# A hashed-attention and maxout feed-forward kernel: bits issued from GpSimd's queue, new due units for the reciprocal chain, feed-forward from unit 11, weight parts from unit 2

## The chip, the cores and the metric

The kernel runs on one core of one Trainium2 chip. The metric is the device time of one execution in microseconds (us). A core has TensorE (PE: matmuls, and PEld: loading their weights), VectorE (DVE), ScalarE (ACT), GpSimd (POOL) and SyncE (SP, which here only issues DMAs). Each engine works its instructions off in the order in which the program gives them. A DMA issued by SP or by POOL waits in that engine's queue until what it waits for is there, and everything behind it in the same queue waits too.

## The reference

Attention with a hash mask over 4 batches of 8 heads, sequence 768, head size 64; then a feed-forward layer with the maximum of three products.

```python
q_bits = (np.einsum('bhsd,dk->bhsk', q, proj) > 0)        # 6 bits, k_bits likewise
mask = q_bucket[:, :, :, None] == k_bucket[:, :, None, :]  # equal bits
scores = np.where(mask, scale * np.matmul(q, k.transpose(0, 1, 3, 2)), -1e9)
attn = softmax(scores)
x = np.matmul(attn, v)            # then to (B * S, H * D) = (3072, 512)
h = np.maximum(np.maximum(x @ w1, x @ w2), x @ w3)         # 512 -> 768
out = h @ w_out                                            # 768 -> 512
```

## The kernel before, in words

**Pairs and units.** Heads are worked in 16 pairs (`pi`), four to a batch; `jj` is the pair's place in its batch. A pair has 12 units, so a batch has 48 and the kernel 192. A unit (`scores`, L271) is two matmuls (L276) over 128 keys each and one exponential on ACT (L279). The mask is part of the matmul: below the 64 rows of the head lie 6 rows of bits as +0.5 or -0.5 in `S`, so that pairs with unequal bits get a large negative term.

**Preparing a pair** (`prep_groups`, L132). Four `tgroup`s transpose k and q on TensorE (L149) and copy them to `T2` (L157, L159). The first of a pair also issues the k and q loads of the next pair on POOL (`begin`, L114). `hashes` multiplies by `proj` (L193), makes `bits` on DVE (L196) and issues four DMAs that put the bits into `S` (L202). POOL then casts the even half of `S` (L205, `even`), DVE the odd half (L208). Pair 0 has its own way: `hash_first` (L178) and `bits_first` (L181), where DVE writes the bits into `S` without a DMA. Preparation goes on some units ahead: the hashes of pairs 2 to 6 fall on units 15, 26, 35, 45 and 56, and are used from units 23, 35, 47, 59 and 71.

**The values and the reciprocal chain.** After a pair's half (6 units) or whole (12 units), `values` (L302) multiplies by v (L298), sums the exponentials (L312), and DVE writes `avs` and `ys` (L321, L323). The sums must be inverted and spread over partitions, by `normalize` (L329), in four steps: `gather` (SP, L344, `dd<-ys`) at once, then `invert` (DVE L347 and L348, then SP L349, `rd<-rr`), `spread` (SP L353, `rb<-rd`, two DMAs) and `scale` (POOL L357, `xT<-avs,rb`). The last three come due so many units later, as a list of (units, step) says. A step is put into the program at the end of its due unit. What is left after unit 191 is sorted by its due number and placed among the last feed-forward groups, by a running count `at` of their costs.

**Feed-forward** (`ffn_groups`, L216). A batch gives 36 groups of four matmuls (L226, cost 0.66; DVE takes the maximum, L231 and L233) and 6 groups of six matmuls (L239, cost 1.32; ACT copies, L249, SP stores, L250). The first half of the groups reads the first query half of `xT`, all four pairs of it. The groups of batch b start `FFN_AT` units into batch b + 1, at 0.66 a unit; the last batch's come behind the loop.

**Other orders of the loop.** v is loaded on POOL (L121) and cast there (L124). The 15 weight parts are issued on POOL one at a time (L391) at units 8, 12, ..., 64.

Of the kernel before, what the change touches and what calls it, by code (L numbers as in the profile page):

```python
# [12 lines left out]
AluOp = mybir.AluOpType  # L13
# [4 lines left out]
def kernel(  # L18
# [12 lines left out]
    nc = tc.nc  # L31
    B, H, S, D = q.shape
    NBITS = proj.shape[1]
    P = 128
    NCH = S // P

    HALF = S // 2
# [4 lines left out]
    NPAIR = B * HPAIR  # L42
    KR = D + NBITS
# [64 lines left out]
    def load(pi, eng):  # L108
        b, jj = divmod(pi, HPAIR)
        nats = [nat.tile([P, 2, NCH * D], FP32, tag=nm, name=nm) for nm in ("qnat", "knat")]  # L110
        for h0, nh in ((0, 1), (1, 1)) if pi == 0 else ((0, 2),):
            for side in (1, 0):
                h = 2 * jj + h0
                eng.dma_start(nats[side][:, h0 : h0 + nh, :],  # L114
                                  (q, k)[side][b, h : h + nh].rearrange("h (p c) d -> p h (c d)", p=P))
        natural[pi] = nats
# [9 lines left out]
    weight_parts = []  # L126
# [5 lines left out]
    def prep_groups(pi):  # L132
        st = {}

        def begin():
            st["T2"] = t2pool.tile([P, 2, 2, HALF], FP32, tag="T2", name="T2")
            st["S"] = spool.tile([KR, 2, 2, 2, HALF], BF16, tag="S", name="S")
            trans[pi] = st["S"]
            if 1 < pi + 1 < NPAIR:
                load(pi + 1, nc.gpsimd if pi > 1 else nc.sync)  # L140

        def tgroup(side, hd):
            def go():
                if not st:
                    begin()
                mp = ms_ps.tile([P, 512], FP32, tag="ms", name="mp")
                n = natural[pi][side]
                for i in range(CH2):
                    nc.tensor.transpose(mp[:, i * P : (i + 1) * P], n[:, hd, 2 * i * D : (2 * i + 2) * D], iden[:])  # L149
                o = st["T2"][:, side, hd, :]  # L150
                if pi == 0 and (hd, side) != (0, 1):
                    if side == 0:
                        nc.scalar.mul(o, mp[:, 0:HALF], QS)
                    else:
                        nc.scalar.copy(o, mp[:, 0:HALF])
                elif side == 0:
                    nc.vector.tensor_scalar(out=o, in0=mp[:, 0:HALF], scalar1=QS, scalar2=None, op0=AluOp.mult)  # L157
                else:
                    nc.vector.tensor_copy(o, mp[:, 0:HALF])  # L159
                if pi == 0:  # L160
                    nc.gpsimd.tensor_copy(st["S"][0:D, side, hd, 0, :], o[0:D])
            return go

        def odd_first(hd):
            for side in (1, 0):
                o, i_ = st["S"][0:D, side, hd, 1, :], st["T2"][D : 2 * D, side, hd, :]
                if hd == 0:
                    nc.scalar.copy(o, i_)
                else:
                    nc.vector.tensor_copy(o, i_)  # L170

        first_bp = {}

        def hash_first(hd):
            for side in (1, 0):
                bp = first_bp[side] = ms_ps.tile([P, 512], FP32, tag="ms", name="bp")
                for par in range(2):
                    nc.tensor.matmul(bp[32 * par : 32 * par + 32, 0:HALF], pj[:, 1 + par, :], st["T2"][:, side, hd, :],  # L178
                                     start=True, stop=True)

        def bits_first(hd):  # L181
            for side in (1, 0):
                for par in range(2):
                    nc.vector.tensor_scalar(out=st["S"][D:KR, side, hd, par, :],
                                            in0=first_bp[side][32 * par : 32 * par + NBITS, 0:HALF],
                                            scalar1=0.0, scalar2=0.5, op0=AluOp.is_gt, op1=AluOp.subtract)

        def hashes():
            bp = ms_ps.tile([P, 512], FP32, tag="ms", name="bp")
            for side in range(2):  # L190
                for hd in range(2):
                    g = 2 * side + hd
                    nc.tensor.matmul(bp[32 * g : 32 * g + 32, 0:HALF], pj[:, 0, :], st["T2"][:, side, hd, :],  # L193
                                     start=True, stop=True)
            bits = bpool.tile([P, HALF], BF16, tag="bits", name="bits")
            nc.vector.tensor_scalar(out=bits[:], in0=bp[:, 0:HALF], scalar1=0.0, scalar2=0.5,  # L196
                                    op0=AluOp.is_gt, op1=AluOp.subtract)
            for hd in range(2):
                for side in (1, 0):
                    p0 = 32 * (2 * side + hd)  # L200
                    eng = nc.gpsimd if pi == 1 and hd == 1 else nc.sync
                    eng.dma_start(st["S"][D:KR, side, hd, :, :], bits[p0 : p0 + 2 * NBITS, :])  # L202

        def even():
            nc.gpsimd.tensor_copy(st["S"][0:D, :, :, 0, :], st["T2"][0:D])  # L205

        def odd(side):
            return lambda: nc.vector.tensor_copy(st["S"][0:D, side, :, 1, :], st["T2"][D : 2 * D, side])  # L208

        if pi == 0:  # L210
            return [tgroup(1, 0), tgroup(0, 0), lambda: odd_first(0), lambda: hash_first(0), lambda: bits_first(0),
                    tgroup(1, 1), tgroup(0, 1), lambda: odd_first(1), lambda: scores(0), lambda: scores(1),
                    lambda: hash_first(1), lambda: bits_first(1)]
        return [tgroup(s, h) for h in (0, 1) for s in (1, 0)], hashes, [even, odd(1), odd(0)]

    def ffn_groups(b):  # L216
# [45 lines left out]
    UPB = NU // B  # L262
    UPG = NCH
    UPP = 2 * UPG
    WEIGHTS_AT = 8
    FFN_AT = 13
    EARLY_CH = 4
    PAIRS_AT = UPB + UPP
    xts, avs_of, ys_of = {}, {}, {}
# [59 lines left out]
    def normalize(pi, q0, nq):  # L329

        b, jj = divmod(pi, HPAIR)
        if jj == 0:
            xts[b] = xpool.tile([P, NJC, S], FP16, tag="xT", name="xT")
        xt, avs, ys = xts[b], avs_of[pi], ys_of[pi]
        G = 16
        W = nq * HALF // G
        dd = small.tile([2 * G, 2, 2 * HALF // G], FP32, tag="dd", name="dd")
        rr = small.tile([2 * G, 2 * HALF // G], FP32, tag="rr", name="rr")
        rd = drp.tile([2 * G, W], FP32, tag=f"rd{nq}", name="rd")
        rb = rbpool.tile([P, 2, HALF], FP32, tag="rb", name="rb")  # L340

        def gather():
            for half in range(2):
                nc.sync.dma_start(dd[:, half, 0:W], ys[32 * half : P : D, q0 : q0 + nq, :])  # L344

        def invert():
            nc.vector.tensor_add(rr[:, 0:W], dd[:, 0, 0:W], dd[:, 1, 0:W])  # L347
            nc.vector.reciprocal(rr[:, 0:W], rr[:, 0:W])  # L348
            nc.sync.dma_start(rd[:, :], rr[:, 0:W])  # L349

        def spread():
            for hd in range(2):
                nc.sync.dma_start(rb[hd * D : (hd + 1) * D, 0:nq, :],  # L353
                                    rd[hd * G : (hd + 1) * G, :].rearrange("(o p) i -> o (p i)", o=1).to_broadcast((D, nq * HALF)))

        def scale(i):
            return lambda: nc.gpsimd.tensor_mul(xt[:, jj, (q0 + i) * HALF : (q0 + i + 1) * HALF],  # L357
                                                avs[:, q0 + i, :], rb[:, i, :])

        gather()  # L360
        if nq == 1:
            return [(7, invert), (10, spread), (15, scale(0))] if pi < NPAIR - 1 else [(4, invert), (4, spread), (4, scale(0))]
        return [(8, invert), (11, spread)] + [(18, scale(i)) for i in range(nq)]

    with tc.manual_schedule():
        wm = ms_ps.tile([P, 512], FP32, tag="ms", name="wm")
# [16 lines left out]
        for u in range(NU):  # L383
            pi = units[u][0]
# [2 lines left out]
                cast_v[pi + 1] = load_v(pi + 1, nc.gpsimd)  # L387
            if u % UPP == 10 and pi + 1 < NPAIR:
                cast_v[pi + 1]()
            if u >= WEIGHTS_AT and u % 4 == WEIGHTS_AT % 4 and weight_parts:  # L390
                nc.gpsimd.dma_start(*weight_parts.pop(0))  # L391
            if ub == FFN_AT and b > 0:
                ffn += ffn_groups(b - 1)
# [7 lines left out]
            else:  # L401
                fill = slot in (2, 3, 5) if u < UPB + FFN_AT else slot in (1, 4)
            if fill:
                if hash_ready and u < PAIRS_AT:
                    do_hash()
                elif prep and prep[0][0] < pi + AHEAD:
                    _, i, g, hs = prep.pop(0)
# [25 lines left out]
        at = 0  # L433
# [35 lines left out]
```

## Time and profile before

| What | Value |
|---|---|
| Median of 3 runs | 315.08 us (312.65 to 316.27) |
| The profiled execution's own time | 314.91 us |
| Its span, first to last instruction | 313.1 us |
| PE, ACT, DVE, POOL busy | 291.7, 182.4, 195.6, 109.9 us |
| Mean granted TensorE clock | 0.978 |
| DMA | 35.88 MB, mean 115 GB/s |

The span is the time on which the rows of the profile lie; the profiled execution took 1.8 us more than it. A row of a timeline has the start in us, the length in us, the engine, the line, the operation, what it writes and reads, how many instructions were merged, and in brackets how long the engine stood idle before it and for whom. The granted clock is the share of full speed at which TensorE was allowed to run. A row "SPq" or "POOL ... DMA_DIRECT2D" is the issue of a DMA, not its transfer.

### The profile page before, as it was taken

The numbers are of one execution on the slowest core, as the hardware profiler recorded it, in microseconds if no ns is written. First come the engines' busy times: TensorE is split into PE (matmuls) and PEld (weight loads), VectorE is DVE, ScalarE is ACT, GpSimd is POOL, SyncE is SP. The second block draws the span as 40 slices with busy tenths as digits, with TensorE's granted clock in tenths as the row PEclk, the third lists the DMA queues.
The fourth block names the chain that finished last, engine by engine and source line by source line (L and its number), as shares of the span: only waits on it lengthen the run. The fifth ranks groups of instructions, "written<-read, shape, count | busy, mean of one in ns | idle before, by whom it ended". The sixth has DMA issues, their size and how long they took to land.

```text
span 313.1 us, 6752 instructions
## 1 busy us (share of the span) xinstructions
PE 291.7 (93%) x2593; PEld 161.8 (52%) x2593; DVE 195.6 (62%) x419; ACT 182.4 (58%) x222; POOL 109.9 (35%) x131
## 2 busy tenths in 40 slices
PE   8999989895999999999999999999999999469994
PEld 3454445442565566555656566555655555236562
DVE  2867557765478387746876497836763558038481
ACT  3787888882565946584757756683849572200201
POOL 2387545686707061215617070235130200130000
PEclk9999999997799999999999999999999999969999
DMA  7548779397924432245415440233111300410202
GB/s 206 197 89 230 155 160 224 81 250 196 244 85 137 146 122 67 56 144 166 158 51 159 153 129 33 55 98 115 53 54 56 104 2 17 129 61 0 103 0 100
DMA packets 19491, 35.88 MB, mean 115 GB/s; under 512 B 4960, under 2 KB 11700, under 8 KB 19460
## 3 DMA queue, kind: packets, MB, share of 16 engines
q0 software_dynamic: 7200, 19.29, 22.7%
q1 hardware_dynamic: 11956, 16.04, 16.5%
q8 instruction: 20, 0.33, 0.4%
q10 hardware_dynamic: 304, 0.13, 0.2%
q14 instruction: 11, 0.09, 0.1%
HBM read 31.46 MB, written 6.39 MB: 121 GB/s over the span
## 4 chain that ended last, share of the span: by engine, by line
PE 76%; DMA 9%; ACT 5%; DVE 3%; issue 2%; SPq 2%; POOL 1%; POOLq 0%; ACTq 0%; DVEq 0%
PE l L226 28%; PE sc L276 17%; PE av L298 9%; PE l L239 7%; PE mp L149 5%; ACT AT L279 4%; PE sm L312 4%; DMA S<-bits 3%; PE bp L193 3%; DMA rd<-rr 3%; DMA rb<-rd 2%; PE wm L368 1%; SPq L353 1%; PE bp L178 1%; SPq L202 1%
## 5 line engine op out<-in xcount | busy, mean ns | idle before, releaser
L279 ACT ACTIVATE AT<-sc,bias_t 128x768 f16<-128x768 f32 x192 | 167.3, 905 | 75.0 <-PE sc L276 70.8
L226 PE MATMUL l<-xT,w_sb 128*128 128x384 f16 x576 | 113.7, 333 | 10.4 <-POOL xT L357 9.7
L276 PE MATMUL sc<-S 70*128 70x384 bf16 x384 | 91.6, 328 | 5.4 <-ACT AT L279 4.3
L226 PEld LDWEIGHTS <-w_sb 128*128 128x128 f16 x576 | 57.0, 99 | 48.7 <-issue 15.1
L357 POOL TENSOR_TENSOR xT<-avs,rb 128x384 f16<-128x384 f32 x32 | 31.7, 1005 | 142.9 <-DMA rb<-rd 120.6
L233 DVE TENSOR_TENSOR ht<-ht,l 128x384 f16<-128x384 f16 x96 | 52.7, 549 | 17.8 <-PE l L226 13.2
L276 PEld LDWEIGHTS <-S 70*128 70x128 bf16 x384 | 34.5, 98 | 44.1 <-issue 24.6
L231 DVE CAST ht<-l 128x384 f16<-128x384 f32 x48 | 26.6, 553 | 30.1 <-PE l L226 29.1
L249 ACT COPY osb<-l 128x512 f32<-128x512 f32 x23 | 13.6, 589 | 45.6 <-PE l L239 45.2
L298 PE MATMUL av<-AT,vo 128*32 128x385 f16 x768 | 38.9, 329 | 0.0
L239 PE MATMUL l<-wout_sb,ht 128*128 128x512 f16 x144 | 34.0, 379 | 0.0
L298 PEld LDWEIGHTS <-vo 128*32 128x32 f16 x768 | 17.5, 96 | 17.5 <-issue 9.8
L205 POOL CAST S<-T 64x1536 bf16<-64x1536 f32 x15 | 22.0, 1466 | 12.6 <-DVE T L157 12.6
L157 DVE TENSOR_SCALAR T<-mp 128x384 f32<-128x384 f32 x30 | 16.5, 549 | 14.2 <-PE mp L149 13.7
L159 DVE COPY T<-mp 128x384 f32<-128x384 f32 x31 | 17.2, 554 | 12.7 <-PE mp L149 11.5
L208 DVE CAST S<-T 64x768 bf16<-64x768 f32 x30 | 21.7, 731 | 0.5
L239 PEld LDWEIGHTS <-ht 128*128 128x128 f16 x144 | 14.0, 97 | 15.0 <-DVE ht L233 0.4
L312 PE MATMUL sm<-AT,ones 128*32 128x384 f16 x384 | 21.1, 325 | 0.0
L321 DVE TENSOR_SCALAR avs<-av,sv 128x384 f32<-128x384 f32 x32 | 19.8, 618 | 1.6
L323 DVE TENSOR_SCALAR ys<-sm 128x384 f32<-128x384 f32 x32 | 17.5, 548 | 0.0
L149 PE MATMUL mp<-iden,knat 128*128 128x128 f32 x96 | 16.3, 279 | 0.3 <-DMA knat<-in_k_dram 0.2
L149 PE MATMUL mp<-iden,qnat 128*128 128x128 f32 x96 | 16.1, 277 | 0.1
(42 smaller groups left out, 157.0 us busy)
## 6 DMA issues: line engine op xcount, KB each, us to landing
out_dram<-osb SPq DMA_DIRECT2D x23, 256.0 KB
vnat<-in_v_dram POOLq DMA_DIRECT2D x15, 384.0 KB, 4.4
knat<-in_k_dram POOLq DMA_DIRECT2D x13, 384.0 KB, 4.3
qnat<-in_q_dram POOLq DMA_DIRECT2D x13, 384.0 KB, 4.7
rb<-rd SPq DMA_DIRECT2D x24, 192.0 KB
w_sb<-in_moe_w_dram POOLq DMA_DIRECT2D x12, 192.0 KB, 5.8
rb<-rd SPq DMA_DIRECT2D x16, 96.0 KB
S<-bits SPq DMA_DIRECT2D x58, 9.0 KB
```

The lines of the kernel that those rows point to most:

```text
L149: nc.tensor.transpose(mp[:, i * P : (i + 1) * P], n[:, hd, 2 * i * D : (2 * i + 2) * D], iden[:])
L205: nc.gpsimd.tensor_copy(st["S"][0:D, :, :, 0, :], st["T2"][0:D])
L208: return lambda: nc.vector.tensor_copy(st["S"][0:D, side, :, 1, :], st["T2"][D : 2 * D, side])
L226: nc.tensor.matmul(ps[:, 0:HALF], w_sb[wi][:, jc, fb * P : (fb + 1) * P], xb[:, jc, hf * HALF : (hf + 1) * HALF], start=(jc == 0), stop=(j ...
L231: nc.vector.tensor_copy(hts[fb][:], ps[:, 0:HALF])
L233: nc.vector.tensor_tensor(out=hts[fb][:], in0=hts[fb][:], in1=ps[:, 0:HALF], op=AluOp.max)
L239: nc.tensor.matmul(ps[:, 0:DM], hts[fb][:, tb * P : (tb + 1) * P], wout_sb[:, fb, :], start=(fb == 0), stop=(fb == NFB - 1))
L276: nc.tensor.matmul(sc[:, j, 0:HALF], th[0:KR, 1, hd, j, kp * P : (kp + 1) * P], th[0:KR, 0, hd, qh, :], start=True, stop=True)
L279: nc.scalar.activation(at[:, :, 0:HALF], sc[:, :, 0:HALF], ActFn.Exp, bias=bias_t[:], scale=SCALE)
L298: nc.tensor.matmul(av[p0 : p0 + 32, 0 : HALF + 1], vones[pi][:, hd, d0 : d0 + 32], at[:, c % 2, 0 : HALF + 1], start=(c == 0), stop=(c == ...
L312: nc.tensor.matmul(sm[32 * t : 32 * t + 32, 0:HALF], ones[:, :], at_of(qh, hd, c)[:, c % 2, 0:HALF], start=(s == 0), stop=(s == CH2 - 1))
L357: return lambda: nc.gpsimd.tensor_mul(xt[:, jj, (q0 + i) * HALF : (q0 + i + 1) * HALF], avs[:, q0 + i, :], rb[:, i, :])
```

## The change

The bits of a pair go out on POOL's queue instead of SP's, except those of pair 1's first head. In `bits_first` the four operations become six, the k side cut at column 128, in another order. The due units of the chain depend on the pair's place: 4, 7, 11 for the last pair of a batch (was 7, 10, 15), 4, 6, 8 for the last pair of all (was 4, 4, 4), 8, 13, 18 for the first two of a batch and 6, 9, 14 for the third (both were 8, 11, 18). Feed-forward starts at unit 11 of the next batch instead of 13; the same constant moves the unit from which preparation takes fewer slots, from 61 to 59. The weight parts go at units 2, 4, 6, 8, then 12 to 52 by 4.

```diff
         def bits_first(hd):
-            for side in (1, 0):
-                for par in range(2):
-                    nc.vector.tensor_scalar(out=st["S"][D:KR, side, hd, par, :],
-                                            in0=first_bp[side][32 * par : 32 * par + NBITS, 0:HALF],
-                                            scalar1=0.0, scalar2=0.5, op0=AluOp.is_gt, op1=AluOp.subtract)
+            for side, par, lo, hi in ((1, 0, 0, P), (1, 1, 0, P), (0, 0, 0, HALF), (1, 0, P, HALF), (1, 1, P, HALF),
+                                      (0, 1, 0, HALF)):
+                nc.vector.tensor_scalar(out=st["S"][D:KR, side, hd, par, lo:hi],
+                                        in0=first_bp[side][32 * par : 32 * par + NBITS, lo:hi],
+                                        scalar1=0.0, scalar2=0.5, op0=AluOp.is_gt, op1=AluOp.subtract)
...
-                    eng = nc.gpsimd if pi == 1 and hd == 1 else nc.sync
+                    eng = nc.sync if pi == 1 and hd == 0 else nc.gpsimd
                     eng.dma_start(st["S"][D:KR, side, hd, :, :], bits[p0 : p0 + 2 * NBITS, :])
...
-    WEIGHTS_AT = 8
-    FFN_AT = 13
+    WEIGHTS_AT = (2, 4, 6, 8) + tuple(range(12, 56, 4))
+    FFN_AT = 11
...
         if nq == 1:
-            return [(7, invert), (10, spread), (15, scale(0))] if pi < NPAIR - 1 else [(4, invert), (4, spread), (4, scale(0))]
-        return [(8, invert), (11, spread)] + [(18, scale(i)) for i in range(nq)]
+            return [(4, invert), (6, spread), (8, scale(0))] if pi == NPAIR - 1 else [(4, invert), (7, spread), (11, scale(0))]
+        at = (8, 13, 18) if jj < 2 else (6, 9, 14)
+        return [(at[0], invert), (at[1], spread)] + [(at[2], scale(i)) for i in range(nq)]
...
-            if u >= WEIGHTS_AT and u % 4 == WEIGHTS_AT % 4 and weight_parts:
+            if u in WEIGHTS_AT:
                 nc.gpsimd.dma_start(*weight_parts.pop(0))
```

## The prediction

> **What bounds the kernel now.** I read the page first, then the busy time by stage, then the chain that ended last, and the timelines of POOL and of the DMA queues around the two places where the chain leaves TensorE.
>
> ```profile
> span 313.1 us, 6752 instructions
> PE 291.7 (93%) x2593; PEld 161.8 (52%) x2593; DVE 195.6 (62%) x419; ACT 182.4 (58%) x222; POOL 109.9 (35%) x131
> PEclk9999999997799999999999999999999999969999
> ```
>
> TensorE is the engine to beat, and its clock falls twice, near 72 to 86 us and near 274 to 281 us. By stage (PE, PEld, DVE, ACT, POOL busy, granted clock, DMA share, GB/s):
>
> ```profile
> 9.20:72.00 62.80, 58.49 (x623) 29.01 (x624) 43.30 (x88) 52.56 (x64) 41.01 (x51) 1.00 0.69 170
> 76.00:262.00 186.00, 184.32 (x1716) 107.28 (x1719) 122.03 (x255) 120.73 (x144) 61.77 (x67) 0.98 0.33 102
> 73.00:76.00 3.00, 0.20 (x3) 0.01 (x1) 1.12 (x3) 0.00 (x0) 1.05 (x2) 0.80 0.84 287
> 76.00:81.50 5.50, 5.50 (x18) 2.63 (x18) 2.18 (x4) 0.90 (x1) 4.12 (x6) 0.50 0.66 152
> 269.50:276.90 7.40, 0.53 (x4) 0.23 (x3) 0.41 (x2) 0.58 (x1) 2.03 (x3) 0.72 0.28 99
> ```
>
> There are four stages. In 9 to 72 us (units 0 to 60, no feed-forward) ScalarE paces at about 1.02 us a unit, and DMA and POOL are well filled. In 76 to 262 us TensorE is full at 1.43 us a unit. Between them lies a hole of 3 us, and a second of 7 us stands before the last feed-forward. Who ends the holes:
>
> ```profile
> 74.95 0.98 POOL L357 TENSOR_TENSOR xT<-avs,rb 128x384 f16<-128x384 f32 x1 [2.59 <-DMA rb<-rd]
> 75.98 3.04 PE L226 MATMUL l<-xT,w_sb 128*128 128x384 f16 x9 [2.81 <-POOL xT L357]
> ...
> 267.45 0.99 POOL L357 TENSOR_TENSOR xT<-avs,rb 128x384 f16<-128x384 f32 x1 [17.40 <-DMA rb<-rd]
> 274.87 2.89 POOL L357 TENSOR_TENSOR xT<-avs,rb 128x384 f16<-128x384 f32 x3 [6.42 <-DMA rb<-rd]
> 276.86 3.44 PE L226 MATMUL l<-xT,w_sb 128*128 128x384 f16 x12 [6.87 <-POOL xT L357]
> ```
>
> Both end with a scale on POOL. The second is an order, not a latency: pair 14's two scales are due 18 units after unit 180, six past the loop's end, while pair 15's second chain is due at 4. So POOL holds pair 14's scales behind pair 15's second half (the x3 at 274.87), and TensorE starts at 276.86, when the second of the three ends (274.87 + 2 x 0.96 = 276.8).
>
> **Part 1, the tail (-7.9 us).** With 6, 9, 14 pair 14 is inverted at unit 186, spread at 189 and scaled at 2 past the loop, and pair 15's first half is spread at 0 and scaled at 2; the second half follows at 4, 6, 8. POOL's order is now 14, 14, 15 first half, 15 second half. What is late next is pair 15's first half, because its spread stands on SP behind the gather of the second half, which waits for the last values. Two units more of feed-forward are done inside the loop, so three instead of five 0.65 us groups remain behind those values: their sums end at about 263.7 (262.4 + 1.3), ys 1.0 later, two gathers (0.6 each) to 266.0, spread, landing 3.5 later (row: issue 271.34, POOL at 274.87) at 269.5, scale 0.99. TensorE runs dry at 269.5 + 3 x 0.163 = 270.0 and goes on at about 270.5: 0.5 us of hole instead of 6.87. The slow clock goes too: the chain has 11 matmuls of line 226 in 3.28 us from 276.86, at full speed 11 x 0.163 = 1.79, so 1.5. Sum 6.87 + 1.5 - 0.5 = 7.9. Bounds: 8.4 without a hole; 5.0 if the landing takes 4.7 (the 70.13 us row of rb) and the clock drops again. The second half is needed only 18 x 0.65 + 3 x 1.3 = 15.6 us later, and that covers its later steps; without the cover 4, 6, 8 would cost up to 4 units of 1 us.
>
> **Part 2, bits on POOL.** 56 of 58 issues leave SP, four a pair:
>
> ```profile
> 16.95 1.17 POOL L202 DMA_DIRECT2D S<-bits  x2 [4.80 <-DVE bits L196]
> 27.64 3.18 SPq L202 DMA_DIRECT2D S<-bits  x4
> 30.09 4.64 DMA S<-bits
> 39.88 5.79 DMA S<-bits
> ```
>
> SP gains 3.2 us a pair; POOL pays 4 x 0.585 = 2.35. The issue on POOL waits for DVE's bits, and behind it in POOL's queue stand the even cast, the next pair's k and q loads, weight parts and the next scale. The bits landed 4.6 and 5.8 us after the issue on SP, with 0.8 us of TensorE waits; the two on POOL took 1.9 to 2.3. Behind earlier loads in POOL's own queue I take 2 to 4 us, in time for units 23 and 35, so -0.8 (bounds -0.8 to +0.6). In the full stage POOL waits 9 us a pair for rb, which hides all of it.
>
> The Trainium skill's page "DMA: Bandwidth & Descriptors" (Issuing engine by pattern) speaks against this: a simple transfer belongs on Sync, since GpSimd builds its descriptors in software, and its first byte is put at about 1 us against 0.6. By that rule alone each bits transfer would land some 0.4 us later, an estimate from that page, still hidden by 8 units; the rows above show the reverse, in a quieter moment.
>
> The price is in the loads. Laying POOL's first stage out again by its rows: bits(2) 27.6 to 29.95, cast to 31.4, w, loads(4) 32.0; bits(3) 38.5 to 40.85, cast, loads(5) 42.3; two scales to 46.5, w and v cast, bits(4) 48.4 to 50.75, v, w, cast, loads(6) 53.5 (before 49.12). The scales of pair 1 still end at 59.2 to 60.0, since their rb still lands near 57.5: spread(1) now stands behind gather(2) on SP, 50.6 against 50.89. Then w, bits(5) to 62.15, cast, cast, loads(7) 64.5:
>
> ```profile
> 62.71 0.72 POOL L114 DMA_DIRECT2D knat<-in_k_dram  x1
> 67.71 0.55 PE L149 MATMUL mp<-iden,knat 128*128 128x128 f32 x3 [0.24 <-DMA knat<-in_k_dram]
> ```
>
> That load was just late already. k lands in 3.4 to 5.5 us (median 4.3). Loads(6) are there at 58.5 for unit 47 at 58.0: +0.3 with its slack. Loads(7) at 69.4 for unit 57 at 67.7: +1.7.
>
> **Part 3, the boundary (-4.6 us, with those two stalls).** Pair 3's first half: invert at 46, spread 49, scale 53 (were 49, 52, 57); pair 2: 42, 45, 50. With SP free of 3.2 us of bits at 58.53, spread(2) issues near 59.5 (was 61.83), rd of pair 3 near 61 (was 64.48), spread near 64 (was 69.55). POOL, with its queue, scales pair 2 from 67.3 and pair 3 at 69.8 to 70.8. Feed-forward starts at unit 59, at 72.5 - 2.0 = 70.5 without stalls (71.87 + 0.6 of other waits was unit 61), 72.5 with 0.3 + 1.7. So POOL's scale is in time. Compare at the start of unit 61's feed-forward: before, 75.98 plus the slow clock (18 matmuls in 5.5 us, 2.9 at full speed: 2.6) = 78.6; after, 72.5 plus the other TensorE work of two units (1.43 - 0.66 = 0.77 each) = 74.0. Gain 4.6. Bounds: 6.6 without stalls; -1 if k takes the longest 5.5 and q 6.6, the hole is as long as before and the clock drops again.
>
> Whether 1.7 us of hole costs clock: the trace has holes under 0.6 us at clock 1.00 and one of 2.81 us followed by 5.5 us at 0.50. I take no loss: 1.7 lies midway, and it is split over a k and a q wait with work between them. The page "TensorE: Matmul & The Clock Gate" (HAM oscillation) says that idle gaps up to about 3.4 us are safe; this trace differs, since 2.81 us dropped it. By the page alone a hole of 3 us would keep the clock; by the row it costs 2.6.
>
> **Part 4, small ones.** First bits: from sv (128x1, 160 ns) and 384 columns (549 ns), 1.02 ns a column; 128 take 290 and 256 take 420, so six cost 2.5 against 2.2. The first scores are ready 0.5 us earlier, but ScalarE is still copying T until 9.65, so nothing is won; DVE runs without a gap from 10.86 to 15.12 ahead of pair 1's hash: +0.3 (bounds 0 to +0.6). Weights at 2 and 4 fall into POOL's 4.80 us wait, when DMA moved 81 GB/s (10 to 20 us); the last three parts leave 68.7 to 81 us, where the share is 1.04. Free; without that wait 0.58 each on POOL. Spread at 13 instead of 11 for the first two pairs of a batch: consumed at unit 59 or 107, 0. Feed-forward two units earlier in the full stage moves the output copies (0.59 us on ScalarE) against the values: TensorE waits of 0.62 there can go or come, 0 +- 1.5.
>
> **Sum.** -7.9 - 4.6 - 0.8 + 0.3 = -13.0. The profiled execution took 314.91 (span 313.1, 1.8 around it), beside a median of 315.08. 314.9 - 13.0 = **302.0 us**.
>
> **Rivals.** (a) POOL's detour costs nothing, the loads land in time: -8.4 - 6.6 - 0.8 + 0.3 gives 299.5. For it: SP's hops shorten and DMA is quieter at 57 to 64. Against: the load at 62.71 was already late. 0.13. (b) The boundary's hole only changes its owner, from rb to k and q, clock drop included: -7.9 alone with the small ones at about 0, 307.0. For it: POOL is full in 58 to 66 us. 0.19. (c) Slower: POOL paces the first stage. Its work a pair becomes 2.35 + 1.46 + 1.5 + 0.72 + 1.7 + 0.85 + 1.96 = 10.5 of about 12 us; with waits of 4.6 and 6.4 us for rb as before it needs 15 to 17, and if loads lose all their lead, five pairs lose 3 to 5 us, some 15 to 20, against 7.9: 322 to 327. It decides once a pair loses over 1.6 us. Against: 8 to 12 units of lead. 0.04. (d) The last scales still wait on the gather or nothing moves: 311 to 315. 0.02. Forecast 0.62.
>
> A measurement of this kernel can tell about 1% from no change. Faster by that (below 311.9) holds in (a), (b) and the forecast, less their worst ends: 0.92; same 0.05; slower 0.03. Range 298.0 to 308.5, from (a)'s best to past (b).
>
> **What would show it.** Right: POOL's last scales as x3 near 265 to 270 and a hole under 1 us; clock 1.00 from 270; bits as POOL L202 of 0.58; rb of pair 3 landing before 69; a wait of TensorE for knat near 58 and 68. Wrong: a hole of over 2 us at the tail, a clock drop near 70, or more than 1 us of waits for k and q at three or more pairs.

## The result: 319.6 us, slower by 1.1%

| | Before | After |
|---|---|---|
| Median of 17 runs each | 315.99 us (312.65 to 320.43) | 319.62 us (315.88 to 322.23) |
| Ratio, 95% interval | | 1.0112 (1.0071 to 1.0153) |
| Profiled execution, span | 314.91 us, 313.1 us | 319.98 us, 317.9 us |

The forecast was 302.0 us, and the range of 298.0 to 308.5 does not hold the result. The page of the changed kernel, with the chain that ended last and two groups of instructions:

```profile
span 317.9 us, 6742 instructions
PE 293.2 (92%) x2593; PEld 162.2 (51%) x2593; DVE 214.3 (67%) x423; ACT 183.1 (58%) x222; POOL 140.8 (44%) x187
...
PEclk9999999986999999999999999996999999999999
...
PE 69%; DVE 11%; DMA 5%; issue 5%; ACT 4%; POOL 4%; SPq 0%; ACTq 0%; POOLq 0%
PE l L226 26%; PE sc L276 14%; PE av L298 9%; PE l L239 6%; DVE S L208 6%; PE mp L149 5%; PE sm L312 4%; ACT AT L279 4%; PE bp L193 3%; DVE ht L233 2%; DMA dd<-ys 2%; DMA knat<-in_k_dram 2%; POOL S L202 1%; PE wm L369 1%; DMA rd<-rr 1%
...
L202 POOL DMA_DIRECT2D S<-bits x58 | 33.6, 584 | 87.5 <-DVE bits L196 84.9
...
L208 DVE CAST S<-T 64x768 bf16<-64x768 f32 x30 | 38.4, 1288 | 0.8
```

The bits are issued as predicted: 58 issues of 0.58 us on POOL. But DVE is busy for 18.7 us more, and 16.7 of them belong to one line whose work was not changed, the odd cast L208. It now has 6% of the chain. The same two views of the kernel before:

```profile
PE 76%; DMA 9%; ACT 5%; DVE 3%; issue 2%; SPq 2%; POOL 1%; POOLq 0%; ACTq 0%; DVEq 0%
...
L208 DVE CAST S<-T 64x768 bf16<-64x768 f32 x30 | 21.7, 731 | 0.5
```

By stage in the changed kernel (columns as in the prediction: start and end, length, PE, PEld, DVE, ACT and POOL busy, granted clock, DMA share, GB/s):

```profile
9.20:72.00 62.80, 54.38 (x568) 26.53 (x566) 39.82 (x85) 49.10 (x59) 48.95 (x66) 0.98 0.73 183
76.00:262.00 186.00, 176.07 (x1626) 102.44 (x1626) 134.56 (x240) 114.95 (x137) 80.88 (x102) 0.98 0.32 99
68.00:71.50 3.50, 0.55 (x4) 0.19 (x6) 1.24 (x5) 0.83 (x2) 0.16 (x2) 0.74 1.10 215
72.00:76.00 4.00, 4.00 (x27) 1.59 (x25) 2.42 (x5) 1.80 (x2) 2.91 (x6) 0.50 0.17 56
270.00:285.00 15.00, 14.67 (x113) 7.93 (x110) 9.83 (x22) 5.36 (x7) 3.60 (x4) 1.00 0.29 95
```

In 76 to 262 us TensorE was busy for 184.32 of 186 us before, and now for 176.07: the stage that was full has holes. The boundary still has its hole (68 to 71.5) and its slow clock (72 to 76). Only the tail, 270 to 285 us, is as forecast.

To see where time goes in each kernel, two marks serve that all of them have: the start of the hash matmuls (L193) of unit 72 and of unit 168. They split the span into what lies before unit 72, the full stage of 96 units, and the rest.

| Kernel | to unit 72 | 72 to 168 | 168 to end | Span | Median | Ratio to before, 95% |
|---|---|---|---|---|---|---|
| before | 95.0 | 137.3 | 80.8 | 313.1 | 315.99 | |
| after | 96.6 | 149.6 | 71.7 | 317.9 | 319.62 | 1.0112 (1.0071 to 1.0153) |
| a1_bits_sp | 96.9 | 137.9 | 72.2 | 307.0 | 309.17 | 0.9827 (0.9769 to 0.9884) |
| a2_even_first | 93.8 | 139.8 | 72.4 | 306.0 | 308.24 | 0.9781 (0.9713 to 0.985) |
| b1_bits_pool | 93.5 | 170.0 | 81.6 | 345.1 | 347.61 | 1.1013 (1.0944 to 1.1081) |
| b2_due_units | 94.0 | 136.5 | 72.9 | 303.5 | 304.36 | 0.9603 (0.953 to 0.9675) |
| e4_pool_waits | 93.0 | 148.0 | 82.9 | 323.9 | 325.25 | 1.0292 (1.0229 to 1.0354) |
| g2_after_odd_act | 97.4 | 146.0 | 73.4 | 316.8 | 317.50 | 1.0034 (0.9984 to 1.0084) |
| g1_c1_odd_act | 92.7 | 146.0 | 73.2 | 311.9 | 315.00 | 0.9937 (0.9902 to 0.9972) |
| c1_even_first_late | 91.9 | 138.0 | 72.4 | 302.3 | 306.20 | 0.9728 (0.9654 to 0.9803) |
| c2_due_units_late | 92.4 | 136.7 | 72.7 | 301.8 | 303.71 | 0.9618 (0.9547 to 0.9689) |
| e1_wout_after | 91.6 | 137.9 | 72.4 | 301.9 | 305.42 | 0.9671 (0.9579 to 0.9762) |
| f1_even_first_ffn13 | 89.5 | 146.1 | 72.6 | 308.2 | 309.25 | 0.9775 (0.9703 to 0.9848) |
| d1_due_ffn11 | 93.6 | 138.1 | 72.6 | 304.3 | 307.22 | 0.9731 (0.9658 to 0.9803) |
| e2_tail_only | 93.1 | 136.9 | 72.5 | 302.5 | 306.90 | 0.969 (0.9612 to 0.9768) |
| d2_due_weights | | | | | 304.15 | 0.9634 (0.956 to 0.9709) |

The medians are of all executions, slow ones included, while the ratios compare fast executions alone, each with the kernel before run beside it, whose median lay between 314.75 and 317.09 us. Of d2_due_weights the times alone are used. Two cautions on the columns. Where feed-forward starts two units earlier (after, a1, a2, c1, e1, g1, g2, d1), two groups of four matmuls more lie ahead of unit 72 (64 matmuls of that line instead of 56), 8 x 0.163 = 1.3 us, and as many fewer behind unit 168. And the first column scatters by about 2 us between executions: e2_tail_only is the same as before up to there and shows 93.1 against 95.0.

So the change lost 1.6 us ahead of unit 72, lost 12.3 in the full stage and won 9.1 behind it: +4.8, the difference of the spans. Of the 12.3 us, TensorE stood still for 8.3 (149.6 us with 139.8 busy, against 137.3 with 135.8); the other 4.0 are the same matmuls run longer, while its clock was low.

### The profile page after: what moved, and what is told of

It is laid out like the page before. It is cut to its first block, busy times and chain, and to the rows that moved or that the text cites. A ratio compares the mean times of both kernels' runs of the same rounds, so it can differ in the third digit from the quotient of the medians.

```text
span 317.9 us, 6742 instructions
## 1 busy us (share of the span) xinstructions
PE 293.2 (92%) x2593; PEld 162.2 (51%) x2593; DVE 214.3 (67%) x423; ACT 183.1 (58%) x222; POOL 140.8 (44%) x187
## 4 chain that ended last, share of the span: by engine, by line
PE 69%; DVE 11%; DMA 5%; issue 5%; ACT 4%; POOL 4%; SPq 0%; ACTq 0%; POOLq 0%
PE l L226 26%; PE sc L276 14%; PE av L298 9%; PE l L239 6%; DVE S L208 6%; PE mp L149 5%; PE sm L312 4%; ACT AT L279 4%; PE bp L193 3%; DVE ht L233 2%; DMA dd<-ys 2%; DMA knat<-in_k_dram 2%; POOL S L202 1%; PE wm L369 1%; DMA rd<-rr 1%
## 5 line engine op out<-in xcount | busy, mean ns | idle before, releaser
L226 PE MATMUL l<-xT,w_sb 128*128 128x384 f16 x576 | 111.5, 328 | 4.5 <-DVE ht L231 4.2
L276 PE MATMUL sc<-S 70*128 70x384 bf16 x384 | 93.2, 333 | 4.8 <-ACT AT L279 4.6
L226 PEld LDWEIGHTS <-w_sb 128*128 128x128 f16 x576 | 56.3, 98 | 41.8 <-issue 7.7
L202 POOL DMA_DIRECT2D S<-bits x58 | 33.6, 584 | 87.5 <-DVE bits L196 84.9
L233 DVE TENSOR_TENSOR ht<-ht,l 128x384 f16<-128x384 f16 x96 | 52.9, 551 | 14.7 <-PE l L226 9.0
L208 DVE CAST S<-T 64x768 bf16<-64x768 f32 x30 | 38.4, 1288 | 0.8
L298 PEld LDWEIGHTS <-vo 128*32 128x32 f16 x768 | 17.8, 97 | 19.0 <-issue 11.6
L205 POOL CAST S<-T 64x1536 bf16<-64x1536 f32 x15 | 22.5, 1500 | 0.0
L149 PE MATMUL mp<-iden,knat 128*128 128x128 f32 x96 | 16.7, 283 | 0.7 <-DMA knat<-in_k_dram 0.3
```

The costliest lines, as they stand in the source:

```text
L226: nc.tensor.matmul(ps[:, 0:HALF], w_sb[wi][:, jc, fb * P : (fb + 1) * P], xb[:, jc, hf * HALF : (hf + 1) * HALF], start=(jc == 0), stop=(j ...
L233: nc.vector.tensor_tensor(out=hts[fb][:], in0=hts[fb][:], in1=ps[:, 0:HALF], op=AluOp.max)
L276: nc.tensor.matmul(sc[:, j, 0:HALF], th[0:KR, 1, hd, j, kp * P : (kp + 1) * P], th[0:KR, 0, hd, qh, :], start=True, stop=True)
L298: nc.tensor.matmul(av[p0 : p0 + 32, 0 : HALF + 1], vones[pi][:, hd, d0 : d0 + 32], at[:, c % 2, 0 : HALF + 1], start=(c == 0), stop=(c == ...
```

## Experiments: which part costs it

The theories, as the expectations call them. **P**: the bits' issue holds POOL until DVE has made the bits, so that POOL's even cast (L205), next in its queue, starts just when DVE does the odd cast (L208). The two then run side by side, and DVE's cast is held. **M**: what bounds the boundary is the traffic of 60 to 72 us, whoever issues it. Other readings of the loss are the DMAs themselves on POOL, and the due units or the earlier feed-forward.

**The bits back on SP, all else changed (a1).**

```diff
-                    eng = nc.sync if pi == 1 and hd == 0 else nc.gpsimd
+                    eng = nc.gpsimd if pi == 1 and hd == 1 else nc.sync
```

> The changed kernel with the bits issued by SP again, all else as changed. Theory P (port): the four bits issues on POOL cost little themselves; they hold POOL's even cast back until it runs at the same time as VectorE's odd cast (L208), and VectorE's cast is held for as long as POOL computes (5.56 us with L205, L357 x3 behind each other). P expects L208 back from 38.4 us to about 22, the full stage between the hashes of units 72 and 168 back from 149.6 to about 137.5, and 306 to 309 us. Rival Q (feed-forward order): the loss comes from starting feed-forward at unit 11, which puts the output groups elsewhere; Q expects 318 to 321, unchanged. Rival D (descriptors): the DMA issues on POOL themselves slow VectorE; D also expects 306 to 309 here.

The full stage returned from 149.6 to 137.9 us, and L208 from 38.4 to 19.5 us (659 ns each). All but 0.6 us of the loss there goes with the queue of the bits. What is left ahead of unit 72 is not it.

**The even cast ahead of the bits' issues in POOL's queue (a2).** The bits stay on POOL.

```diff
         def hashes():
+            even()
...
-        return [...], hashes, [even, odd(1), odd(0)]
+        return [...], hashes, [lambda: None, odd(1), odd(0)]
```

> The changed kernel, bits still on POOL, but POOL's even cast put ahead of them in its queue, so that it runs before the bits are ready, as in the kernel before. P expects L208 back near 22 us and 306 to 310 us, like the run with the bits on SP. D expects L208 and the time to stay near 38 us and 319. Q expects 319 too, with L208 lower.

139.8 us in the full stage, L208 at 25.0 us. The same DMAs from the same queue cost little once the even cast no longer stands behind them.

**The bits on POOL alone, and the due units alone, each in the kernel before (b1, b2).** b1 takes the line of L201 from the change; b2 takes `normalize`'s lists and nothing else.

> The kernel before with nothing but the bits on POOL. P and D expect the loss without the gain of the tail: L208 35 to 45 us, 325 to 331 us. Q expects 314 to 317, no change.

> The kernel before with nothing but the new due units of the reciprocal chain. The tail's step of the prediction expects the hole of 6.87 us at 270 us and its slow clock gone: 307 to 308 us, or 304 if the hole at 73 us goes as well. A second loss (V), that VectorE stands still in its queue at the invert of unit 52 because the gather has not landed, would show as a wait of 2 to 5 us of L347 near 65 us and leave the hole near 72 us in place under another name: 307 to 309.

b1 is 10% slower: 32.7 us more in the full stage, and L208 takes 44.1 us. The loss is larger than in the changed kernel, and larger than the forecast of 325 to 331 us. In the full stage TensorE is busy for 147.7 of 170.0 us, so that it stands still for 22.3 us instead of 1.5, and its work takes 11.9 us longer, at a clock that falls again and again behind holes of 2 to 3 us. DVE, POOL and TensorE in one such place of b1 (a part of the rows):

```profile
119.14 4.41 DVE L208 CAST S<-T 64x768 bf16<-64x768 f32 x1
...
119.41 1.48 POOL L205 CAST S<-T 64x1536 bf16<-64x1536 f32 x1
...
120.84 1.93 POOL L357 TENSOR_TENSOR xT<-avs,rb 128x384 f16<-128x384 f32 x2
...
122.73 0.97 POOL L114 DMA_DIRECT2D knat<-in_k_dram  x1
...
124.19 1.44 PE L226 MATMUL l<-xT,w_sb 128*128 128x384 f16 x4 [3.02 <-DVE ht L233]
```

The cast is held for as long as POOL computes, 119.41 to 122.77, and ends at 123.55 while POOL is issuing a load. Behind it in DVE's queue is the maximum (L233), and TensorE waits 3.02 us for that. b2, the due units alone, is the fastest thing so far: 4.0% faster than before.

**The same wait without moving a DMA (e4).** The bits stay on SP, but POOL reads one column of them ahead of the even cast:

```diff
+            look = small.tile([P, 1], BF16, tag="look", name="look")
+            nc.gpsimd.tensor_copy(look[:], st["bits"][:, 0:1])
             nc.gpsimd.tensor_copy(st["S"][0:D, :, :, 0, :], st["T2"][0:D])
```

> The kernel before, bits on SP and no DMA moved; POOL only copies one column of the bits ahead of its even cast, so that the even cast waits for the bits as it does behind the bits issues. P expects VectorE's odd cast to be held as with the bits on POOL: L208 35 to 45 us instead of 21.7 and 325 to 348 us. D (the DMA issues on POOL slow VectorE) and Q expect 314 to 318.

It costs 2.9%, 10.7 us in the full stage, though not one DMA was moved. The odd cast takes 36.9 us in all, and both this and the time are at the lower end of what P expected. The casts of e4 (its lines stand two lower; L210 is the odd cast, L207 the even one, L359 the scale):

```profile
114.27 0.19 POOL L206 COPY look<-bits 128x1 bf16<-128x1 bf16 x1 [13.26 <-DVE bits L196]
...
114.40 1.46 POOL L207 CAST S<-T 64x1536 bf16<-64x1536 f32 x1
...
115.58 2.61 DVE L210 CAST S<-T 64x768 bf16<-64x768 f32 x1
...
115.83 1.94 POOL L359 TENSOR_TENSOR xT<-avs,rb 128x384 f16<-128x384 f32 x2
...
118.71 0.81 PE L228 MATMUL l<-xT,w_sb 128*128 128x384 f16 x4 [1.14 <-DVE ht L233]
```

So the order on POOL costs by itself, without the issuing of the bits.

**The odd cast taken off DVE (g2, g1).** For pairs 7 to 15 ACT does it, in the changed kernel (g2) and in c1 (g1; c1 is told below: the even cast first, and one more edit at the boundary).

```diff
-            return lambda: nc.vector.tensor_copy(st["S"][0:D, side, :, 1, :], ...)
+            return lambda: (nc.scalar.copy if pi > 6 else nc.vector.tensor_copy)(st["S"][0:D, side, :, 1, :], ...)
```

> The changed kernel as it is, bits on POOL and the even cast behind them, but the odd casts of pairs 7 to 15 on ScalarE instead of VectorE. POOL is as late as in the changed kernel; only the instruction that is held is gone. P expects the full stage between the hashes of units 72 and 168 back from 149.6 to 137 to 140 us and 306 to 310 us. If POOL's lateness costs in another way (S too late for the scores, loads, scales), it stays at 316 to 320.

> The changed kernel with the even cast first, the late second half, and the odd casts of pairs 7 to 15 on ScalarE. P expects what is left of held casts there (L208 at most 2.5 us, 20.5 us in all) to be worth nothing: 304.5 to 307, as the 306.2 without it; ScalarE has the room (69% in that stage).

With the cast on DVE, POOL's two orders differ by 149.6 - 138.0 = 11.6 us in the full stage. With it on ACT, they take 146.0 both. The group in g2:

```profile
L208 ACT CAST S<-T 64x768 bf16<-64x768 f32 x18 | 14.9, 830 | 0.4
```

ACT's cast is the same 830 ns in g2 and 831 in g1, whatever POOL does. P's forecasts were missed in both: 137 to 140 and 306 to 310 us were expected of g2 and 304.5 to 307 of g1, where 146.0 and 317.5, and 315.0, came out. They had put the casts on ACT at nothing, and these cost some 8 us against c1's 138.0, so as a remedy it is none. g2 by itself is in the range that was written for the other reading, a cost of POOL's lateness as such. What speaks for P is the pair: with the cast off DVE, TensorE stands still for 7.7 us of the stage in g2 and in g1 alike, and POOL's order makes no difference. DVE is still held in g2, in another instruction, the first add of the invert, which takes 0.17 us alone; three scales and the cast of v run beside it, and no time is lost by it:

```profile
139.72 3.20 DVE L347 TENSOR_TENSOR rr<-dd 32x24 f32<-32x24 f32 x1
```

**The boundary (c1, c2, e1).** In the changed kernel TensorE stands still at 68 us, before feed-forward starts:

```profile
70.12 0.17 DVE L347 TENSOR_TENSOR rr<-dd 32x24 f32<-32x24 f32 x1 [5.03 <-DMA dd<-ys]
...
71.08 1.50 PE L193 MATMUL bp<-T,pj 128*32 128x384 f32 x6 [2.95 <-DVE sv L320]
...
71.41 0.99 POOL L357 TENSOR_TENSOR xT<-avs,rb 128x384 f16<-128x384 f32 x1 [3.34 <-DMA rb<-rd]
...
76.54 2.12 PE L226 MATMUL l<-xT,w_sb 128*128 128x384 f16 x12
```

The first row is the invert of the second half of the batch's last pair, due 4 units after its gather where it was due 7. DVE waits 5.03 us there for the gather to land, and the values' first operation (L320), for which TensorE waits, stands behind it. c1 is a2 with that half's three steps 6 units later; c2 is b2 with the same edit:

```diff
-            return ... else [(4, invert), (7, spread), (11, scale(0))]
+            return ... else [(n + 6 * (q0 == 1), f) for n, f in ((4, invert), (7, spread), (11, scale(0)))]
```

> The changed kernel with the even cast ahead of the bits on POOL's queue, and the second half of a batch's last pair inverted, spread and scaled 6 units later (10, 13, 17); its scale is first read 24 units after feed-forward starts. Theory V (VectorE stands at unit 52's invert for the gather, and TensorE behind it) expects the wait of L347 near 67 us to go and 304 to 306 us, 3 us under the run without the late half. Rival M (memory): the transfers of 60 to 72 us set the boundary, VectorE only shows it; M expects the wait to move to another instruction and the time to stay at 308.

> The kernel before with the new due units alone, and the second half of a batch's last pair 6 units later. There the wait of L347 was 3.85 us and the chain went through the gather's landing (4.04 us). V expects it gone and 300 to 302 us. M expects 304.

DVE's wait is gone, and another has come, as M expects. In c1 (a line lower than after):

```profile
70.05 0.65 PE L227 MATMUL l<-xT,w_sb 128*128 128x384 f16 x3
...
71.26 0.98 POOL L358 TENSOR_TENSOR xT<-avs,rb 128x384 f16<-128x384 f32 x1 [2.42 <-DMA rb<-rd]
...
72.30 1.62 PE L227 MATMUL l<-xT,w_sb 128*128 128x384 f16 x9 [1.59 <-POOL xT L358]
```

Feed-forward starts at 70.05 instead of 76.54, with the three matmuls that don't need the last scale, and goes on at 72.30, after a hole of 1.59 us that keeps the clock. In c2 the hole is 1.70 us, for `xT` too. By time, c2 against b2 is no difference (0.9618 and 0.9603), and c1 against a2 is not told apart (0.9728 and 0.9781): the gain of about 3 us that V expected doesn't show. That something ahead of unit 72 is worth time shows in g2 and g1, which take the same 146.0 us in the full stage: 97.4 against 92.7 us to unit 72, and ratios of 1.0034 and 0.9937 whose intervals are apart. The two differ in the late half and, in pairs 1 to 6, in the even cast's place; the runs don't divide it between these.

For M, e1 takes c1 and moves the last three weight parts out of the stretch, to units 64, 68 and 72:

```diff
-    WEIGHTS_AT = (2, 4, 6, 8) + tuple(range(12, 56, 4))
+    WEIGHTS_AT = (2, 4, 6, 8) + tuple(range(12, 44, 4)) + (64, 68, 72)
```

> The changed kernel with the even cast first and the late second half, and the last three weight parts (0.77 MB, first read from unit 77 on) moved from units 44 to 52 to units 64, 68 and 72, behind the boundary. M (transfers of 60 to 72 us set the boundary) expects the chain's hops there shorter, the 1.6 us wait on xT at 72 us gone and 303 to 305. If the time stays at 306, the weights are not what fills that window.

The stretch of 66 to 72 us in c1, and then in e1:

```profile
66.00:72.00 6.00, 4.71 (x48) 1.97 (x41) 3.77 (x8) 4.64 (x6) 3.57 (x5) 1.00 1.06 253
```

```profile
66.00:72.00 6.00, 6.00 (x66) 2.67 (x64) 4.50 (x8) 5.42 (x7) 3.42 (x4) 1.00 0.41 124
```

The DMA share falls from 1.06 to 0.41, and TensorE's hole for `xT` is gone. From the issue of the last spread to its scale it takes 4.2 us instead of 6.1 (65.40 to 69.60, and 65.19 to 71.26 in c1): the traffic did hold the last scale, as M says. In part the hole is gone because TensorE came to feed-forward 1.1 us later in this execution, after a stretch at a low clock. The time does not show the gain (0.9671 against 0.9728, intervals that overlap): what the hole held up is no more than what executions differ by.

**Smaller parts (d1, d2, f1).** d1 is b2 with feed-forward from unit 11, d2 is b2 with the new places of the weights, f1 is c1 with feed-forward back at unit 13.

> The kernel before with the new due units and feed-forward from unit 11, nothing else. The prediction's step expects -0.5 to 0 us: 303.5 to 305. Theory Q' (starting at 59 puts the first feed-forward behind a scale that is not there yet) expects a wait on xT near 72 us and 306 to 309, which would account for the 4.8 us between the changed kernel with bits on SP and the due units alone.

> The kernel before with the new due units and the new places of the weight parts, nothing else. The prediction's step costs them at nothing: 303.5 to 305. The other account of the 4.8 us (three parts more in POOL's queue and in the transfers ahead of unit 52 make loads, gathers and scales of the first stage late) expects 306 to 309.

> The same with all as changed but the even cast first, the late second half and feed-forward from unit 13 again. If starting at 59 costs the 2 to 3 us that the two runs with and without it differ by (304.4 and 307.2), this gives 303 to 304; if it costs nothing, 306.

d2 equals b2: the weights are free, as forecast. d1 is 2.9 us above b2 in the medians, with intervals that overlap. That is the range of Q', but not its cause: in d1 feed-forward starts at 73.55 us without a wait for `xT`. f1 went the other way than d1: its full stage takes 146.1 us instead of c1's 138.0, though its median lies only 3 us higher and the intervals overlap. In its trace (a line lower than after) TensorE stands still for 7.0 us of that stage instead of 2.0, most of it in two holes of 2.24 and 3.00 us, each behind an odd cast that is held. The first of these casts:

```profile
127.66 3.62 DVE L209 CAST S<-T 64x768 bf16<-64x768 f32 x1
...
127.95 2.90 POOL L358 TENSOR_TENSOR xT<-avs,rb 128x384 f16<-128x384 f32 x3
```

Here the even cast is out of the way, but three scales stand behind the bits' wait and meet the odd cast instead. So two units of feed-forward shift what meets what. Apart from that they cost little: with 11 instead of 13 the full stage is 1.6 us longer in d1 than in b2 and 1.4 in c1 than in c2.

**The tail alone (e2).** Before, with the new lists for the last two pairs only (6, 9, 14 and 4, 6, 8).

> The kernel before with new due units for the last two pairs alone (6, 9, 14 and for the last 4, 6, 8). The prediction's part 1 expects -7.9: 307 to 308.5, with the wait of 6.87 us gone and the hole at 73 us as before. What the due units alone gave beyond that (304.4) would then be the boundary's share, 3 to 4 us.

0.969: 3.1% (2.3 to 3.9) of 315.99 is 9.8 us (7.3 to 12.3), where 7.9 was forecast; by the trace it is 80.8 - 72.5 = 8.3.

## Why the prediction was wrong, step by step

**Part 1, the tail: right, size included.** b2, with feed-forward at 13 as before, gives it unmixed: 80.8 - 72.9 = 7.9 us, the number predicted. In the changed kernel POOL's order is 14, 14, 15 first half, 15 second half:

```profile
278.51 1.95 POOL L357 TENSOR_TENSOR xT<-avs,rb 128x384 f16<-128x384 f32 x2 [7.86 <-DMA rb<-rd]
...
282.03 1.00 POOL L357 TENSOR_TENSOR xT<-avs,rb 128x384 f16<-128x384 f32 x1 [1.57 <-DMA rb<-rd]
...
283.08 11.37 PE L226 MATMUL l<-xT,w_sb 128*128 128x384 f16 x69 [0.33 <-POOL xT L357]
```

A hole of 0.33 us stands where 0.5 was forecast and 6.87 was, at clock 1.00. (A scale of each half came by itself, not three in a row as the last section of the prediction had it.)

**Part 2, the bits on POOL: this step failed.** The sentence is "In the full stage POOL waits 9 us a pair for rb, which hides all of it." It did hide the issues, 2.3 us a pair, and the bits landed a median 2.5 us after them, within the 2 to 4 forecast. But the prediction had itself listed the even cast behind the waiting issue, and asked only when POOL would be done with it, not beside which instruction of another engine it would now run. One such meeting of the changed kernel:

```profile
133.50 2.29 POOL L202 DMA_DIRECT2D S<-bits  x4 [7.92 <-DVE bits L196]
...
134.58 0.56 DVE L208 CAST S<-T 64x768 bf16<-64x768 f32 x1
...
135.75 5.56 DVE L208 CAST S<-T 64x768 bf16<-64x768 f32 x1
135.80 1.48 POOL L205 CAST S<-T 64x1536 bf16<-64x1536 f32 x1
...
137.23 2.89 POOL L357 TENSOR_TENSOR xT<-avs,rb 128x384 f16<-128x384 f32 x3
...
140.08 0.81 POOL L124 CAST vo<-vnat 128x768 f16<-128x768 f32 x1
...
141.23 0.54 DVE L159 COPY T<-mp 128x384 f32<-128x384 f32 x1
...
141.83 1.46 PE L239 MATMUL l<-wout_sb,ht 128*128 128x512 f16 x6 [2.01 <-DVE T L159]
```

The first odd cast of the pair runs while POOL only issues the bits: 0.56 us. The second begins with the even cast and is held over five POOL instructions in a row, until 141.31: 5.56 us. The copy of the next transposes stands behind it on DVE, and TensorE waits for that. The same meeting comes again at 209.44 us, with the same hole of 2.01 us, and this time the clock falls behind it (TensorE's row, and the stretch that follows):

```profile
215.52 1.85 PE L239 MATMUL l<-wout_sb,ht 128*128 128x512 f16 x6 [2.01 <-DVE T L159]
...
216.50:224.00 7.50, 7.09 (x26) 3.50 (x24) 1.52 (x3) 4.08 (x5) 1.72 (x2) 0.55 0.28 99
```

Not every meeting is so long. Of the eight behind unit 72, four look like this one, where POOL has nothing to do behind the even cast; two casts take 2.70 us and two 5.56:

```profile
117.83 1.94 DVE L208 CAST S<-T 64x768 bf16<-64x768 f32 x1
117.87 1.48 POOL L205 CAST S<-T 64x1536 bf16<-64x1536 f32 x1
```

The pair of 135.75 us before the change, with an odd cast that meets nothing but the end of the scales (and the loads):

```profile
130.93 1.96 POOL L357 TENSOR_TENSOR xT<-avs,rb 128x384 f16<-128x384 f32 x2 [11.63 <-DMA rb<-rd]
...
132.33 0.96 DVE L208 CAST S<-T 64x768 bf16<-64x768 f32 x1
...
133.69 0.55 DVE L208 CAST S<-T 64x768 bf16<-64x768 f32 x1
```

The price was 12.3 us in the full stage, where nothing was put down: 8.3 of waits and 4.0 of low clock. It was there to be read in the trace before: L208's mean of 731 ns beside 550 for an undisturbed cast, and 0.96 beside the scale.

The Trainium skill's page "SBUF — State Buffer" (SBUF: two separate sides; Who interferes with whom) has the rule that the prediction did not draw on: VectorE and GpSimd share one pair of ports, a cast is among the VectorE operations that can take it, and who has it keeps it for a whole instruction while "the other fully blocks". The runs agree on who disturbs whom (DVE's cast by POOL's work, ACT's cast never, 830 and 831 ns). On how long they agree in part: held for the even cast alone, the odd cast would take 1.48 + 0.56 = 2.0 us, an estimate by that page with the rows' durations, and 1.94 or 1.95 is what four meetings took. But where POOL has more work without a gap, DVE's cast does not get in between two of POOL's instructions and takes 5.56. And the page gives the pair to whoever starts first, where DVE's row begins first in the changed kernel (135.75 against 135.80) and in f1 (127.66 against 127.95), and DVE is the one that is held. That it is this pair of ports, no run here shows.

The rest of Part 2: the hashes of units 35 and 45 come at 45.17 and 54.84 us, 1.05 earlier than before, where -0.8 + 0.3 was forecast. The price in the loads was put too high. In the changed kernel the first one came as forecast (in c1 and e1 it was 1.05 and 1.43 us):

```profile
57.67 0.55 PE L149 MATMUL mp<-iden,knat 128*128 128x128 f32 x3 [0.34 <-DMA knat<-in_k_dram]
```

The second, 1.7 us at unit 57, did not come: the load went out at 62.51, not 64.5, and TensorE was held by DVE before it got there.

**Part 3, the boundary: the -4.6 us did not come.** At equal work, unit 72 came at 96.6 - 1.3 = 95.3, against 95.0 before: nothing won. The step asked whether POOL's scale would be in time, for the first half of pair 3, and left out that half's sister: its invert, moved up to 4 units after the gather, waits on DVE for 5.03 us, with the values behind it. The hole was 2.95 us and the clock fell to 0.50, as in the case that the prediction named as its lower bound (-1), but for this gather and not for k and q. Nor was the first half's scale in time: it ended at 72.4 us in the changed kernel and at 72.2 in c1, where 70.8 was forecast. With the second half late, c1's feed-forward goes on at 72.30, where 72.5 was forecast, but by another way: it starts at 70.05 after one stall of 1.05 us for k, where two of 2.0 together were counted, and then waits for the scale. Unit 72 comes at 91.9 - 1.3 = 90.6, 4.4 earlier than before, of 5.1 forecast for all that lies ahead of it (-4.6 - 0.8 + 0.3); against e2's 93.1 it is 2.5. So the gain can be had, but its size lies within the scatter of that column, and the medians of c1 and a2 don't settle it.

**Part 4.** The weights were free. Feed-forward at 11 was put at 0 +- 1.5; it costs 1.4 to 1.6 us of the full stage (d1, c1), and f1 shows 8 us hanging on it the other way, through the collisions. The first bits were not tried by themselves.

**The sum.** Predicted -13.0 (its sums hold to 0.1 us). Measured by spans, with the two groups put back to where they were: tail -9.1 + 1.3 = -7.8, all that lies ahead of unit 72 +1.6 - 1.3 = +0.3, full stage +12.3, together +4.8. Rival (c) had the sign, but not the place: POOL did not pace the first stage, and the loads kept their lead but for 0.34 us.

**The best version.** b2, c2 and d2 beat both kernels, at 304.36, 303.71 and 304.15 us, and are not told apart: in these runs the due units carry the whole gain, and the bits belong on SP or behind the even cast.

## What to carry to other kernels

When an instruction that waits is put into another engine's queue, what is behind it gets a new time of day: ask not only whether that engine has time to spare, but which instruction of the other engines will run beside it now. In this kernel VectorE's casts and GpSimd's computing want to be kept apart, and a group whose mean lies well above its shortest member is the sign that two engines already meet. An earlier due unit for a step that waits for a DMA is an earlier wait for all that stands behind it on its engine, so that the second half of a pair needs its own working, not the first half's.

## What the runs showed of the hardware

A cast on DVE that meets POOL's computing can be held over a whole row of POOL's instructions, 5.56 us where 0.55 is usual, and so can a small add (3.20 us where 0.17 is usual, in g2). The short issues of the bits on POOL don't hold the cast (0.56 us at 134.58, in the midst of four issues). The issues of the larger k and q loads can, by less: in the kernel before, a cast took 0.96 us at 149.71, with two of them and nothing else on POOL beside it.

The length of a hole alone did not decide on TensorE's clock. Holes of 1.59 and 1.70 us kept clock 1.00, and one of 2.95 us was followed by 0.50, as the 2.81 us before. But of the two holes of 2.01 us in the changed kernel, the one at 141.8 us kept 1.00 and the one at 215.5 did not, and in e1 the clock fell behind a hole of 1.43 us:

```profile
59.02 0.55 PE L149 MATMUL mp<-iden,knat 128*128 128x128 f32 x3 [1.43 <-DMA knat<-in_k_dram]
...
60.00:66.00 6.00, 6.00 (x56) 3.37 (x49) 4.94 (x10) 4.28 (x6) 5.60 (x8) 0.72 0.63 183
```

So the prediction's choice to count 1.7 us as free, because it lies midway, was not safe.
